# Fourier mixing and SwiGLU in one kernel: the two filter products of batches 2 to 7 summed on GpSimd before the middle inverse, and their mixing spread over 125 slots

## The chip, the cores and the metric

The kernel runs on one core of one Trainium2 chip. The metric is the time of one execution on the device, in microseconds (us). Before the change it took 990.07 us (median of three runs, 989.37 to 992.18).

The engines are named as in the profile. PE is the matmul engine, and PEld its weight loads. DVE is VectorE, ACT is ScalarE, POOL is GpSimd, and SP is SyncE. SP only issues DMA transfers here. The program gives each engine its instructions in an order, and in the traces here an instruction that has to wait, or a long one, holds up what stands behind it: in the changed kernel a copy on DVE starts at 596.56 us, when the 0.69 us operation placed ahead of it has ended.

## The reference, cut to what matters

```python
def _attn_ref(x, filt_r, filt_i):            # x: 8 x 3008 x 256
    X = np.fft.rfft(x, axis=1)
    F = (filt_r + 1j * filt_i)[None, :, :]
    return np.fft.irfft(X * F, n=x.shape[1], axis=1).astype(np.float32)

def _moe_ref(x, w_gate, w_val, w_out, rms_g): # x: 24064 x 256, d_ff 1536
    rms = np.sqrt(np.mean(x * x, axis=-1, keepdims=True) + 1e-06)
    xn = x / rms * rms_g
    g = xn @ w_gate
    silu = g * (1.0 / (1.0 + np.exp(-g)))
    return (silu * (xn @ w_val) @ w_out).astype(np.float32)
```

The first function mixes the 3008 tokens of each batch with a filter in the frequency domain. The second is an RMS norm and a gated feed-forward network on every token.

## The kernel before

The transform of length 3008 = 47 x 64 is done as small matmuls in fp16. One batch passes through these stages, named by the PSUM tile that PE writes:

- `psa`: first forward stage. ACT copies it out, and it is stored to a scratch tensor `z_tmp` in HBM.
- `psb`: second forward stage, from `t2`, which is loaded from `z_tmp`. It has 16 units of two columns of the filter.
- Filter: DVE makes two products of `psb`, `s1` with the real part of the filter and `s2` with the imaginary part.
- `psi`: middle inverse, four matmuls a unit. ACT copies it out, and it is stored to `g_tmp`.
- `psn`: last inverse, from `t4`, which is loaded from `g_tmp`. ACT makes `y` and the square `sq` of it.
- `psq`: row sums of the squares. DVE and POOL turn them into the factor of the norm, and POOL makes `xn`.

```python
def b_unit(b, i):
    ps = bank(0 if b else i % 2, "psb").rearrange("p (a d) -> p a d", a=2)   # bank 0: psM, "mx"
    for u in range(2):
        k = 2 * i + u
        nc.tensor.matmul(ps[:, u, :], wb[:, k, :], st[b]["t2"][k // KC][:, k % KC, :], ...)
    ...
    eng.tensor_tensor(out=s1, in0=ps, in1=f1, op=ALU.mult)     # DVE for b > 0
    eng.tensor_tensor(out=s2, in0=ps, in1=f2, op=ALU.mult)

def bi_unit(b, i):
    ...
    for u in range(2):
        for q in range(2):
            nc.tensor.matmul(ps[:, u, :], wi[:, 2 * i + u, q, :], s12[q][:, u, :],
                             start=(q == 0), stop=(q == 1))
```

The feed-forward part is a stream of 576 slots: 8 batches x 6 blocks of 512 tokens (the last of a batch has 448) x 12 slices of the hidden width. In a slot `gv` makes `pg` and `pv` (four 512-column matmuls), ACT makes `sg = silu(pg)` and DVE makes `hh = pv * sg`. Two slots later `down` multiplies `hh` into `po`. After the twelfth slice ACT copies one half of `po` out and DVE the other. There is only one pair of `po` buffers.

```python
psG = ...tile_pool(name="psG", bufs=2, ...)    # pg
psV = ...tile_pool(name="psV", bufs=2, ...)    # pv
psO = ...tile_pool(name="psO", bufs=1, ...)    # po0, po1
psM = ...tile_pool(name="psM", bufs=2, ...)    # "mx": psa, psb, psi, psn, psq

def down(b, m, jt):
    ...
    if jt == JT - 1:
        nc.scalar.activation(out=o3[:, 0:2, :], in_=po[0], func=AXT.Copy)
        nc.vector.tensor_copy(out=o3[:, 2:4, :], in_=po[1])          # m < 5
```

The mixing of batch b is laid between the slots of batch b-1 by a plan that says which unit goes into which slot. Inside a slot the order is `gv`, then the planned units, then `down`:

```python
for b in range(1, B):
    t = (b - 1) * 72                                   # first slot of batch b - 1
    a0, b0, bs = (8, 24, 6) if b == 1 else (0, 16, 8)
    ...                                                # a_unit, z_store, t2_load
    for i in range(16):
        s0 = t + b0 + bs * i // 4                      # one psb unit every second slot
        at(s0, b_unit, b, i)
        at(s0 + 3, bi_unit, b, i)
        if i % 2 == 1:
            at(s0 + 4, g_store, b, i // 2)
    for c in range(4):
        at(t + 54, t4_load, b, c)
    for m in range(6):
        norm_plan(b, m, t + 57 + 8 * m)
for i in range(len(items) + 4):
    gv(*items[i])
    for fn, a in plan.get(i, ()):
        fn(*a)
    down(*items[i - 2])                                # guards and o_store cut
```

## Time and profile before

| view | number |
|---|---|
| busy PE, DVE, ACT, POOL (page) | 92%, 60%, 61%, 26% of 988.5 us |
| PE in the stretch 549 to 662 us, one batch | busy 110.8 of 112.8 us, clock 1.00 |
| time from one batch's last output copy to the next's, batches 1 to 6 | 112.6 to 113.8 us |
| one group of four 256-column or two 512-column matmuls (timeline) | 0.434 us to the next |

The page gives the busy time, share of the span and number of instructions of each engine. Its row PEclk cuts the span into 40 slices and gives the granted clock of PE in tenths.

```profile
PE 910.5 (92%) x6287; PEld 576.3 (58%) x6287; DVE 594.6 (60%) x961; ACT 606.1 (61%) x1061; POOL 256.1 (26%) x219
PEclk8557989999999999999999999999999999999999
```

The windows view cuts the span where one batch's last output copy ends and the next one's. Its columns are the window, its length, the busy time of PE, PEld, DVE, ACT and POOL (with instructions), the granted clock, the DMA share and GB/s. Here is one batch of the kernel before:

```profile
549.37:662.18 112.81, 110.84 (x782) 70.87 (x781) 70.97 (x118) 73.25 (x132) 27.74 (x22) 1.00 0.48 112
```

PE is busy for 98% of it, and no other engine for as much as two thirds. The kernel is bound by PE: what PE does not have to do is time gained, and any hole on PE is time lost.

The timeline of PE in the kernel before has the start, the duration, the operation and the count of a group. In square brackets stand the idle time before the group and what ended it. This is a whole slot with a `psi` unit in it:

```profile
500.07 0.60 PE L239 MATMUL psi<-s,wi 128*128 128x256 f16 x4
500.50 0.60 PE L376 MATMUL po<-wo,hh 128*128 128x256 f16 x4
500.94 0.59 PE L360 MATMUL pg<-xn,wg 128*128 128x512 f16 x2
501.37 0.59 PE L360 MATMUL pv<-xn,wv 128*128 128x512 f16 x2
```

The durations overlap; it is the starts that count. The groups start 0.43 us apart, so 0.109 us goes to one 256-column matmul, and a slot takes 1.30 us without mixing work.

The waits of PE in the kernel before have the waiting tile, what it waited for, the total, the number of times and the longest:

```profile
PE psb L213 <- DMA t<-z_tmp: 17.6, 8, 4.8
PE psi L239 <- DVE s L231: 2.6, 6, 0.4
PE po L376 <- DVE o L382: 0.6, 1, 0.6
```

The first `psb` of each batch waits for its load from `z_tmp`; for batches 2 to 7 together that is 9.1 of the 17.6 us.

One hole in batch 1's mixing shows what a long wait costs beyond itself:

```profile
128.16 0.61 PE L213 MATMUL psb<-t,wb 96*128 96x256 f16 x2 [3.67 <-DMA t<-z_tmp]
128.57 1.06 PE L376 MATMUL po<-wo,hh 128*128 128x256 f16 x4
129.42 1.06 PE L360 MATMUL pg<-xn,wg 128*128 128x512 f16 x2
```

After 3.67 us without work the groups start 0.85 us apart instead of 0.43, until 134 us.

Last, the queue of SP in the kernel before:

```profile
519.73 8.42 SPq L256 DMA_DIRECT2D t<-g_tmp  x16
```

Issuing the 16 transfers of a batch's `t4` load keeps SP busy for 8.42 us, and whatever is queued behind them is issued that much later.

### The profile page before, as it was taken

What the parts mean: (1) busy time and instruction counts of PE and PEld (TensorE: products, weight loads), DVE (VectorE), ACT (ScalarE), POOL (GpSimd) and SP (SyncE); (2) the same over time, 40 slices, a digit from 0 to 9 for tenths busy, and PEclk for the clock granted to TensorE, in tenths of its full rate; (3) what the DMA queues carried; (4) which work ended last, traced back from release to release, by engine and by line L of the source; (5) the groups of instructions that cost most, each with busy time, mean ns of one, the idle gap of its engine ahead of it and who ended that gap; (6) DMA issues with size and microseconds to landing.
All of it is one profiled execution on the core that took longest, in us unless ns stands there. A gap on an engine that the chain in (4) does not pass through costs nothing.

```text
span 988.5 us, 17348 instructions
## 1 busy us (share of the span) xinstructions
PE 910.5 (92%) x6287; PEld 576.3 (58%) x6287; DVE 594.6 (60%) x961; ACT 606.1 (61%) x1061; POOL 256.1 (26%) x219
## 2 busy tenths in 40 slices
PE   3447989999999999999999999999999999999997
PEld 1224646665666566665666566665666556666654
DVE  6623468546775477645775467655775467655554
ACT  7334845576656865676656765577656756566543
POOL 3564231033301342032401233031411312023300
PEclk8557989999999999999999999999999999999999
DMA  8869573335632474325723375425724343322211
GB/s 195 145 136 165 123 144 80 110 97 113 152 94 79 113 167 96 102 78 140 154 52 120 94 160 115 109 67 112 163 76 125 88 118 89 99 67 62 44 43 40
DMA packets 94837, 106.98 MB, mean 108 GB/s; under 512 B 17112, under 2 KB 69464, under 8 KB 94560
## 3 DMA queue, kind: packets, MB, share of 16 engines
q1 hardware_dynamic: 85104, 87.92, 34.1%
q0 software_dynamic: 9552, 17.77, 12.1%
q8 instruction: 49, 0.80, 0.3%
q14 instruction: 36, 0.29, 0.1%
q10 hardware_dynamic: 96, 0.20, 0.1%
HBM read 70.62 MB, written 49.90 MB: 122 GB/s over the span
## 4 chain that ended last, share of the span: by engine, by line
PE 75%; DMA 9%; ACT 5%; issue 4%; DVE 2%; POOL 2%; SPq 1%; ACTq 0%; DVEq 0%; POOLq 0%
PE po L376 22%; PE pg L360 21%; PE pv L360 21%; PE psi L239 5%; DMA t<-z_tmp 3%; PE psb L213 3%; DMA fi<-in_filt_i_dram 2%; DMA z_tmp<-t 2%; PE psn L270 2%; ACT sq L277 1%; ACT t L194 1%; PE psa L192 1%; SPq L202 1%; DMA xc<-in_x_dram 1%; ACT y L275 1%
## 5 line engine op out<-in xcount | busy, mean ns | idle before, releaser
L365 DVE TENSOR_TENSOR hh<-pv,sg 128x512 f16<-128x512 f32 (+1 forms) x576 | 390.7, 678 | 330.3 <-ACT sg L364 212.8
L364 ACT ACTIVATE sg<-pg 128x512 f16<-128x512 f32 (+1 forms) x576 | 341.1, 592 | 294.9 <-PE pg L360 274.9
L376 PE MATMUL po<-wo,hh 128*128 128x256 f16 x2304 | 349.8, 273 | 3.2 <-DVE o L382 0.6
L360 PE MATMUL pg<-xn,wg 128*128 128x512 f16 (+1 forms) x1152 | 339.9, 377 | 0.0
L360 PE MATMUL pv<-xn,wv 128*128 128x512 f16 (+1 forms) x1152 | 339.1, 376 | 0.0
L376 PEld LDWEIGHTS <-hh 128*128 128x128 f16 x2304 | 221.0, 98 | 93.2 <-issue 14.9
L345 POOL TENSOR_TENSOR xn<-y,rb 128x1024 f16<-128x1024 f32 x46 | 132.2, 2875 | 313.3 <-DMA rb<-r_tmp 220.8
L360 PEld LDWEIGHTS <-wv 128*128 128x128 f16 x1152 | 113.1, 98 | 132.6 <-issue 3.0
L290 POOL TENSOR_TENSOR rho<-u,mhalf 128x4 f32<-128x4 f32 x48 | 48.8, 1017 | 327.8 <-DVE u L288 327.8
L360 PEld LDWEIGHTS <-wg 128*128 128x128 f16 x1152 | 112.9, 98 | 14.1 <-issue 0.6
L244 ACT ACTIVATE t<-psi 96x512 f16<-96x512 f32 x128 | 75.7, 593 | 32.1 <-PE psi L239 30.5
L239 PEld LDWEIGHTS <-wi 128*128 128x128 f16 x512 | 51.5, 102 | 55.9 <-issue 13.1
L230 DVE TENSOR_TENSOR s<-psb,fr 128x512 f16<-128x512 f32 x112 | 76.3, 681 | 10.3 <-PE psb L213 10.3
L231 DVE TENSOR_TENSOR s<-psb,fi 128x512 f16<-128x512 f32 x112 | 76.2, 680 | 0.0
L275 ACT ACTIVATE y<-psn,gsb 128x512 f32<-128x512 f32 x94 | 65.4, 696 | 9.5 <-PE psn L270 4.1
L213 PE MATMUL psb<-t,wb 96*128 96x256 f16 x256 | 52.6, 292 | 18.6 <-DMA t<-z_tmp 17.6
L239 PE MATMUL psi<-s,wi 128*128 128x256 f16 x448 | 67.3, 273 | 2.6 <-DVE s L231 2.6
L194 ACT ACTIVATE t<-psa 128x512 f16<-128x512 f32 x96 | 58.0, 615 | 5.1 <-PE psa L192 2.7
L277 ACT ACTIVATE sq<-psn 128x512 f16<-128x512 f32 x94 | 56.7, 603 | 0.0
L213 PEld LDWEIGHTS <-wb 96*128 96x128 f16 x256 | 25.2, 105 | 40.3 <-issue 17.5
L192 PE MATMUL psa<-xc,wa 128*128 128x512 f16 x96 | 37.3, 405 | 10.6 <-DMA xc<-in_x_dram 8.9
L270 PEld LDWEIGHTS <-t 128*128 128x128 f16 x376 | 29.2, 99 | 21.0
(55 smaller groups left out, 331.6 us busy)
## 6 DMA issues: line engine op xcount, KB each, us to landing
out_dram<-o SPq DMA_DIRECT2D x88, 256.0 KB, 3.6
z_tmp<-t SPq DMA_DIRECT2D x128, 96.0 KB, 2.2
t<-z_tmp SPq DMA_DIRECT2D x32, 384.0 KB, 5.9
g_tmp<-t SPq DMA_DIRECT2D x64, 192.0 KB, 2.4
t<-g_tmp SPq DMA_DIRECT2D x126, 96.0 KB, 2.5
rb<-r_tmp SPq DMA_DIRECT2D x46, 256.0 KB, 4.0
xc<-in_x_dram POOLq DMA_DIRECT2D x56, 192.0 KB, 6.1
out_dram<-o SPq DMA_DIRECT2D x8, 192.0 KB, 3.0
```

Source lines behind the costliest of these rows:

```text
L194: nc.scalar.activation(out=dst, in_=src, func=AXT.Copy)
L213: nc.tensor.matmul(ps[:, u, :], wb[:, k, :], st[b]["t2"][k // KC][:, k % KC, :], start=True, stop=True)
L230: eng.tensor_tensor(out=s1, in0=ps, in1=f1, op=ALU.mult)
L231: eng.tensor_tensor(out=s2, in0=ps, in1=f2, op=ALU.mult)
L239: nc.tensor.matmul(ps[:, u, :], wi[:, 2 * i + u, q, :], s12[q][:, u, :], start=(q == 0), stop=(q == 1))
L244: nc.scalar.activation(out=st[b]["t3"][c][:, 2 * r:2 * r + 2, :], in_=ps[0:KR], func=AXT.Copy)
L275: nc.scalar.activation(out=y[:, dh, :], in_=ps, func=AXT.Identity, scale=gsb[:, dh:dh + 1])
L345: nc.gpsimd.tensor_tensor(out=xv, in0=yv, in1=rv.unsqueeze(1).to_broadcast([P, 2, 4, P]), op=ALU.mult)
L360: nc.tensor.matmul(ps[:, 0:w], wt[:, dt_, ts(jt, P)], xn[:, dt_, 0:w], start=(dt_ == 0), stop=(dt_ == 1))
L364: nc.scalar.activation(out=sg[:, 0:w], in_=pg[:, 0:w], func=AXT.Silu)
L365: nc.vector.tensor_tensor(out=hh[:, 0:w], in0=pv[:, 0:w], in1=sg[:, 0:w], op=ALU.mult)
L376: nc.tensor.matmul(po[s4 // 2][:, s4 % 2, :], hh[:, ts(s4, P)], wo[:, jt, :], start=(jt == 0 and s4 % 2 == 0), stop=(jt == JT - 1 and s4 % ...
```

## The change

The middle inverse multiplies `s1` by one matrix and `s2` by a second one, which is the first with its two halves of 64 rows exchanged and one sign turned. If the halves of `s2` are exchanged when it is made, and the sign is put into the filter, one matrix serves both, and `s1 + s2` can be formed before the matmul. That takes `psi` from four matmuls a unit to two. DVE has to make `s2` in two crosswise halves of 64 partitions, and POOL does the sum. To give the longer chain room, the mixing of batches 2 to 7 is spread: `psb` comes every fourth slot instead of every second, `psi` six slots after its `psb` instead of three, and from the first `psa` to the last store to `g_tmp` one batch now takes 125 slots. PSUM is divided anew: one "mx" buffer for `psa`, `psi` and `psn`, and one "mb" buffer for `psb` and `psq`, where two "mx" buffers served all five.

The core of the diff (small helpers, batch 0's and the x loads' placing cut):

```diff
-                    wi[HALF + q, 0, 1, qq] = -(gr, gi)[cols][0]
+                    wi[HALF + q, 0, 1, qq] = (gr, gi)[cols][0]
...
-    psM = ctx.enter_context(tc.tile_pool(name="psM", bufs=2, space=bass.MemoryType.PSUM))
+    psM = ctx.enter_context(tc.tile_pool(name="psM", bufs=1, space=bass.MemoryType.PSUM))
+    psB = ctx.enter_context(tc.tile_pool(name="psB", bufs=1, space=bass.MemoryType.PSUM))
...
+            if b > 1:
+                nc.vector.tensor_tensor(out=s1, in0=ps, in1=f1, op=ALU.mult)
+                st[b]["s"][i] = (s1, s2, ps, f2)
+                return
...
+    def swap_unit(b, i, h):
+        s1, s2, ps, f2 = st[b]["s"][i]
+        a, e = slice(HALF * h, HALF * h + HALF), slice(HALF - HALF * h, P - HALF * h)
+        nc.vector.tensor_tensor(out=s2[a], in0=ps[e], in1=f2[e], op=ALU.mult)
+        if h:
+            s = ssp.tile([P, 2, D], FP16, tag="s", name="s")
+            nc.gpsimd.tensor_tensor(out=s, in0=s1, in1=s2, op=ALU.add)
+            st[b]["s"][i] = (s,)
...
-            for q in range(2):
-                nc.tensor.matmul(ps[:, u, :], wi[:, 2 * i + u, q, :], s12[q][:, u, :],
-                                 start=(q == 0), stop=(q == 1))
+            for q in range(n):
+                nc.tensor.matmul(ps[:, u, :], wi[:, 2 * i + u, q, :], ss[q][:, u, :],
+                                 start=(q == 0), stop=(q == n - 1))
...
-            a0, b0, bs = (8, 24, 6) if b == 1 else (0, 16, 8)
+            a_at = ([8 + i for i in range(12)] if b == 1 else
+                    [24 + 2 * i for i in range(12)] if b == 2 else [t - 77 + 4 * i for i in range(12)])
+            b_at = [24 + 3 * i // 2 if b == 1 else t - 20 + 4 * i for i in range(16)]
...
-                at(t + b0 - 3 + c if c < 3 else t + b0 + 8, t2_load, b, c)
+                at(b_at[0] - 3 + c if c < 3 else b_at[4] + 1, t2_load, b, c)
...
+                if b > 1:
+                    at(s0 + 1, swap_unit, b, i, 0)
+                    at(s0 + 2, swap_unit, b, i, 1)
+                lag = 6 if b > 1 else 3
+                at(s0 + lag, bi_unit, b, i)
...
-                at(t + 54, t4_load, b, c)
+                at(b_at[15] + (9 if b > 1 else 8), t4_load, b, c)
-                norm_plan(b, m, t + 57 + 8 * m)
+                norm_plan(b, m, t + 52 + 8 * m if b > 1 else t + 57 + 8 * m, 4, 3)
```

In `bi_unit`, `n` is 1 for batches 2 to 7 and 2 for the first two, which keep the old product. A planned `swap_unit` or `sq_unit` goes to the front of its slot, ahead of the other planned units. Where the text says "swaps" below, it means the two `swap_unit` operations. `norm_plan` now takes the gap between the two halves of `psn` and the lag from the second to `psq`, and `sq` is made one slot after its `psn`.

More of the change, by code (lines that the diff above doesn't have):

```diff
@@ L133 @@
     sp = ctx.enter_context(tc.tile_pool(name="sp", bufs=3))
+    ssp = ctx.enter_context(tc.tile_pool(name="ssp", bufs=2))
     t3p = ctx.enter_context(tc.tile_pool(name="t3p", bufs=3))
@@ L179, in bank @@
     def bank(i, name):
-        pool, tag = ((psM, "mx"), (psG, "pg"), (psV, "pv"))[i]
+        pool, tag = ((psM, "mx"), (psG, "pg"), (psV, "pv"), (psB, "mb"))[i]
         return pool.tile([P, 512], FP32, tag=tag, name=name)
@@ L209, in b_unit @@
     def b_unit(b, i):
-        ps = bank(0 if b else i % 2, "psb").rearrange("p (a d) -> p a d", a=2)
+        ps = bank(3 if b else (0, 1, 3)[i % 3], "psb").rearrange("p (a d) -> p a d", a=2)
         for u in range(2):
@@ L232, in b_unit @@
         st[b]["s"][i] = (s1, s2)
+    def swap_unit(b, i, h):
[6 more added lines that the diff above has]
+            st[b]["s"][i] = (s,)
     def bi_unit(b, i):
-        s12 = st[b]["s"].pop(i)
+        ss = st[b]["s"].pop(i)
         ps = bank(0 if b else 2, "psi").rearrange("p (a d) -> p a d", a=2)
+        n = len(ss)
         for u in range(2):
-            for q in range(2):
-                nc.tensor.matmul(ps[:, u, :], wi[:, 2 * i + u, q, :], s12[q][:, u, :],
-                                 start=(q == 0), stop=(q == 1))
+            for q in range(n):
+                nc.tensor.matmul(ps[:, u, :], wi[:, 2 * i + u, q, :], ss[q][:, u, :],
+                                 start=(q == 0), stop=(q == n - 1))
         c, r = divmod(i, 2)
@@ L266, in n_unit @@
         y = st[b]["y"][m]
-        ps = psM.tile([P, 512], FP32, tag="mx", name="psn")
+        ps = bank(0, "psn")
         for q in range(4):
@@ L276, in n_unit, with sq_unit @@
                              scale=gsb[:, dh:dh + 1])
-        nc.scalar.activation(out=st[b]["sq"][m][:, dh, :], in_=ps, func=AXT.Square)
+        st[b]["sq"][m, dh] = ps
+    def sq_unit(b, m, dh):
+        nc.scalar.activation(out=st[b]["sq"][m][:, dh, :], in_=st[b]["sq"].pop((m, dh)),
+                             func=AXT.Square)
     def q_unit(b, m):
         sq = st[b]["sq"].pop(m)
-        ps = psM.tile([P, 4], FP32, tag="mx", name="psq")
+        ps = psB.tile([P, 4], FP32, tag="mb", name="psq")
         for q in range(4):
@@ L416, in f_dup @@
         nc.vector.tensor_copy(out=fr[c][HALF:P], in_=fr[c][0:HALF])
-        nc.scalar.activation(out=fi[c][HALF:P], in_=fi[c][0:HALF], func=AXT.Copy)
+        nc.scalar.activation(out=fi[c][HALF:P], in_=fi[c][0:HALF], func=AXT.Copy, scale=-1.0)
     def wi_group(g):
@@ L426, in wi_group @@
         nc.scalar.activation(out=wi[:, k, 0, :], in_=ps[:, lo:4, :], func=AXT.Copy, scale=S_INV_B)
-        for p0, sign in ((0, 1.0), (HALF, -1.0)):
+        for p0 in (0, HALF):
             nc.vector.tensor_scalar(out=wi[p0:p0 + HALF, k, 1, :],
-                                    in0=ps[HALF - p0:P - p0, lo:4, :], scalar1=sign * S_INV_B,
+                                    in0=ps[HALF - p0:P - p0, lo:4, :], scalar1=S_INV_B,
                                     scalar2=None, op0=ALU.mult)
@@ L508 @@
         w_load(2)
-        n_unit(0, 1, 0)
-        n_unit(0, 1, 1)
+        for dh in range(2):
+            n_unit(0, 1, dh)
+            sq_unit(0, 1, dh)
         for c in range(NXC):
@@ L517, in at, with norm_plan @@
         def at(slot, fn, *a):
-            plan.setdefault(slot, []).append((fn, a))
-        def norm_plan(b, m, s0):
-            at(s0, n_unit, b, m, 0)
-            at(s0 + 1, n_unit, b, m, 1)
-            at(s0 + 3, q_unit, b, m)
-            at(s0 + 5, rho_move, b, m)
-            at(s0 + 10, xn_unit, b, m)
+            todo = plan.setdefault(slot, [])
+            if fn in (sq_unit, swap_unit) and a[0]:
+                todo.insert(0, (fn, a))
+            else:
+                todo.append((fn, a))
+        def norm_plan(b, m, s0, gap, lag):
+            for dh in range(2):
+                at(s0 + gap * dh, n_unit, b, m, dh)
+                at(s0 + gap * dh + (b > 0), sq_unit, b, m, dh)
+            q0 = s0 + gap + lag
+            at(q0, q_unit, b, m)
+            at(q0 + 2, rho_move, b, m)
+            at(q0 + 6, xn_unit, b, m)
         at(1, q_unit, 0, 1)
@@ L530 @@
         for m in range(2, 6):
-            norm_plan(0, m, 2 + (m - 2) * 9)
+            norm_plan(0, m, 2 + (m - 2) * 9, 2, 2)
         for b in range(1, B):
             t = (b - 1) * 72
-            a0, b0, bs = (8, 24, 6) if b == 1 else (0, 16, 8)
+            a_at = ([8 + i for i in range(12)] if b == 1 else
+                    [24 + 2 * i for i in range(12)] if b == 2 else [t - 77 + 4 * i for i in range(12)])
+            b_at = [24 + 3 * i // 2 if b == 1 else t - 20 + 4 * i for i in range(16)]
             for i in range(12):
-                at(t + a0 + i, a_unit, b, i)
+                at(a_at[i], a_unit, b, i)
                 if i % 3 == 2:
-                    at(t + a0 + i + 1, z_store, b, i // 3)
+                    at(a_at[i] + 1, z_store, b, i // 3)
             for c in range(4):
-                at(t + b0 - 3 + c if c < 3 else t + b0 + 8, t2_load, b, c)
+                at(b_at[0] - 3 + c if c < 3 else b_at[4] + 1, t2_load, b, c)
             for i in range(16):
-                s0 = t + b0 + bs * i // 4
+                s0 = b_at[i]
                 at(s0, b_unit, b, i)
-                at(s0 + 3, bi_unit, b, i)
+                if b > 1:
[3 more added lines that the diff above has]
+                at(s0 + lag, bi_unit, b, i)
                 if i % 2 == 1:
-                    at(s0 + 4, g_store, b, i // 2)
+                    at(s0 + lag + 1, g_store, b, i // 2)
             if b + 1 < B:
                 for c in range(NXC):
-                    at(t + 20 + 4 * c, x_load, b + 1, c)
+                    at(a_at[3 * c + 2] + 1, x_load, b + 1, c)
             for c in range(4):
-                at(t + 54, t4_load, b, c)
+                at(b_at[15] + (9 if b > 1 else 8), t4_load, b, c)
             for m in range(6):
-                norm_plan(b, m, t + 57 + 8 * m)
+                norm_plan(b, m, t + 52 + 8 * m if b > 1 else t + 57 + 8 * m, 4, 3)
         stores = {}
```

## The prediction

> **What bounds the kernel now.** The tensor engine. In the table of equal stretches PE is busy 97 to 99% of every 100 us from 200 to 900 us at granted clock 1.00; DVE 60 to 65%, ACT 61 to 66%, POOL 20 to 28%. In the timeline a slot (one gate/up/down step) takes 1.30 us, with a middle-inverse unit of four matmuls 1.74: PE streams. The repeated hole (waits of PE) is the first psb of each batch waiting for its z_tmp load: 1.8, 1.2, 1.9, 1.0, 1.1, 2.1 us for batches 2 to 7.
>
> **Gains, all on the critical path.** 96 units lose two of four 256-column matmuls: 0.44 us becomes 0.22, in all 192 x 0.109 = 20.9 us. The z stores now run far ahead of the loads: the 9.1 us of psb waits lose their old cause. Sum -30 us.
>
> **Work moved, hidden.** 96 more DVE operations of 0.68 us (+65 us) and 96 POOL adds (estimated 1.25 us, as batch 0's POOL products; +120 us) have room: the add has four slots before its matmul.
>
> **Costs**, paid whole, as PE works in order.
> 1. *t2 behind t4 on the SP queue, batches 3 to 7.* In the instruction order the first t2 load of batch b+1 is issued after the 16 t4 loads of batch b, three slots before psb needs it. Chain from the slot of the last psi: copy out 2.0, g store 2.4, 16 issues 7.4 to 8.4, t2 load 3.4 to 4.4 us: about 16.5 us. The psb is wanted after six slots, 9.1 us. Stall 7.5 us, five times. The Trainium skill, "TensorE: Matmul & The Clock Gate", section "Part 1: The HAM clock gate", says that an idle window of some 3.4 us halves the PE clock; this trace agrees: after a 3.7 us hole at 124 us, matmul groups take 0.85 instead of 0.43 us until 134. Estimated at 2.3 us each. +49 us.
> 2. *One buffer instead of two for "mx", batch 1's norm against batch 2's mixing (slots 57 to 102).* Each of 12 psi units awaits the square of the psn before it, on ACT after silu: about 1.0 us each, +12 us. Six psb follow psq on "mb" and await u on DVE: +6 us. Batch 1's first xn is late on POOL, behind an add: +3 us.
> 3. *Slots 11 to 46:* psa behind psi or psn on "mx": 7 x 0.7 + 3 x 1.5 us and one psb: about +9 us.
> 4. *Later batches:* psq awaits the second swap product, about 0.3 us, 30 times: +8 us.
>
> Sum +87 - 30: about 1047 us; I shade it to 1043.
>
> **What would show each step.** psi matmuls fall from 448 to 256 on s tiles. PE waits: psb on the t2 load, five times 6 to 9 us, each followed by a lower PEclk; psi on ACT sq 12 times about 1 us between 170 and 260 us; psq on DVE. The time between two batches, 112.8 us now, grows to about 119.
>
> **What would make it wrong.** If issuing the t4 loads is faster than in the trace, or the t2 load lands sooner, cost 1 shrinks and the result nears 1000 us. Without cost 1 the others roughly cancel the gain. The half-clock stretches may differ. Slower POOL adds would make psi wait on POOL too.
>
> Predicted 1043 us (1010 to 1065); faster by over 2%: 0.06, within 2%: 0.13, slower: 0.81.

## The result, and the profile after

The changed kernel is correct and takes 1064.65 us (median of four runs, 1063.94 to 1068.52). The kernel before took 989.72 us in the same rounds (four runs, 988.75 to 992.18). The ratio is 1.0761, with a 95% interval of 1.0729 to 1.0794: slower. A ratio is always the mean time of one kernel's fast runs over that of the other's of the same rounds, so it is not quite the ratio of the medians quoted. The profiled execution of the changed kernel is its slowest run, 1068.5 us, with a span of 1066.3 us; its first slot starts at 83.8 us, 3.7 us later than in the profiled run of before, which is not counted as an effect and was not followed up.

The page of the kernel after, with the group of the new operation on POOL (its columns: busy us and mean ns of one, then the idle time before):

```profile
PE 910.7 (85%) x6095; PEld 558.3 (52%) x6095; DVE 679.7 (64%) x1057; ACT 622.0 (58%) x1061; POOL 364.8 (34%) x315
PEclk8567989989998999989998999989999999999999
L246 POOL TENSOR_TENSOR s<-s,s 128x512 f16<-128x512 f16 x96 | 110.5, 1151 | 440.4 <-DVE s L243 399.0
```

PE did 192 matmuls less, as intended, yet its share fell from 92 to 85% of a longer span. DVE grew to 64% and POOL to 34%, so no engine is full. Dips stand in the row of the clock, one in nearly every batch. The sum on POOL takes 1.15 us, a little under the 1.25 that was estimated; the Trainium skill, "GPSIMD Engine Reference", section 3.1, gives about 2.6 cycles an element at 1.2 GHz for such an operation, from which 512 elements would be estimated at 1.11 us, so the trace agrees. No `psi` waits for the sum anywhere in the waits of PE. Nor did POOL's new work slow DVE: one `hh` took 678 ns on average before and 681 after (both pages).

Two windows of the kernel after, one batch and the stretch behind one of the dips:

```profile
615.24:738.69 123.45, 110.16 (x749) 67.83 (x748) 85.21 (x134) 75.35 (x132) 46.08 (x38) 0.96 0.45 102
579.00:584.10 5.10, 5.10 (x19) 2.37 (x17) 2.08 (x3) 1.63 (x3) 0.00 (x0) 0.51 0.62 178
```

A batch takes 123.5 instead of 112.8 us. PE is idle for 13 us of it, against 2. For 5.1 us it has work all the time and gets half its clock.

The waits of PE in the kernel after name the holes:

```profile
PE psb L215 <- DMA t<-z_tmp: 46.6, 8, 7.9
PE po L396 <- DVE o L402: 15.4, 23, 0.7
...
PE psi L255 <- ACT sq L296: 11.0, 13, 1.3
PE psq L304 <- DVE s L243: 9.0, 30, 0.6
PE psb L215 <- DVE u L308: 5.4, 7, 0.9
PE po L396 <- DVE o L405: 3.7, 5, 0.7
PE psa L194 <- ACT t L260: 3.2, 7, 0.5
PE pg L380 <- POOL xn L365: 2.8, 1, 2.8
PE psa L194 <- ACT sq L296: 2.5, 2, 1.3
```

(The line left out is batch 0's, before the stream starts.) Five of the eight waits for `z_tmp` belong to batches 3 to 7: 5.93, 6.97, 6.41, 7.95 and 7.25 us. The queue of SP shows where that of batch 5 comes from:

```profile
564.67 0.32 SPq L263 DMA_DIRECT2D g_tmp<-t  x1
567.08 7.26 SPq L272 DMA_DIRECT2D t<-g_tmp  x16
574.39 1.00 SPq L208 DMA_DIRECT2D t<-z_tmp  x2
```

The 16 loads of batch 4's `t4` need its last `g_tmp` store, and can only begin at 567.08. The load that batch 5's first `psb` needs stands behind them in the same queue and is issued at 574.39. PE meanwhile (timeline of the kernel after):

```profile
571.87 0.39 PE L286 MATMUL psn<-wai,t 128*128 128x128 f16 x4
578.67 0.58 PE L215 MATMUL psb<-t,wb 96*128 96x256 f16 x2 [6.41 <-DMA t<-z_tmp]
579.05 1.06 PE L396 MATMUL po<-wo,hh 128*128 128x256 f16 x4
579.90 1.06 PE L380 MATMUL pg<-xn,wg 128*128 128x512 f16 x2
...
584.52 0.60 PE L380 MATMUL pg<-xn,wg 128*128 128x512 f16 x2
```

From 579.05 to 584.52 it does seven groups. At 0.434 us each they would take 3.04 us, so the slow stretch costs another 2.43 us, and 0.16 more for the `psb` before it. Counted in the same way, the stretches behind the five holes cost 2.0, 2.3, 2.6, 2.0 and 2.2 us. A shorter hole, the one behind batch 1's first `xn`, did it too (same view):

```profile
232.74 1.01 PE L380 MATMUL pg<-xn,wg 128*128 128x512 f16 x2 [2.77 <-POOL xn L365]
233.55 1.06 PE L380 MATMUL pv<-xn,wv 128*128 128x512 f16 x2
```

The second largest line of the waits, `po` on the output copy, is a wait that the kernel before had once. It now comes 28 times (23 for the full blocks, 5 for the last, shorter block of a batch). DVE and PE around the end of a block, in the kernel after:

```profile
595.18 0.62 DVE L385 TENSOR_TENSOR hh<-pv,sg 128x448 f16<-128x448 f32 x1 [0.42 <-PE po L396]
595.84 0.69 DVE L243 TENSOR_TENSOR s<-psb,fi 64x512 f16<-64x512 f32 x1
596.56 0.69 DVE L402 COPY o<-po 128x512 f32<-128x512 f32 x1
597.30 0.38 PE L396 MATMUL po<-wo,hh 128*128 128x256 f16 x2 [0.73 <-DVE o L402]
```

DVE does the product `hh`, then a swap, and only then the copy that frees the one `po` buffer, for which the next block's first `down` waits. A block ends every 12 slots and a swap comes every fourth slot in the same place, so once they meet they always meet: the slot number is 1 modulo 4 for both. The pair of `po` matmuls was due at 596.42 (0.22 us after the pair before it, which started at 596.20), and came at 597.30, 0.88 us late. The wait listed is 0.73. The modelled end of the last matmul before a hole covers its first 0.15 us or so (a 256-column matmul is drawn 0.273 us long, but in the stream the next one starts 0.109 us after it). So about 0.16 us, called the tail below, is added to each PE wait where waits are turned into time.

### Where the time went

The time per batch can be added up in the middle of the run. A later experiment (e7) ran the spread schedule with the old product and with nearly no hole, at 109.6 us a batch. 16 units of two 256-column matmuls less are 3.5 us, which leaves 106.1 us of pure stream.

| part of one batch, batches 2 to 5 | us |
|---|---|
| stream | 106.1 |
| `psb` behind the `t4` loads, 7.1 + 0.16 | 7.3 |
| half clock after it | 2.3 |
| `po` on the output copy, 5 x 0.86 | 4.3 |
| `psq` on the swap, 1.9 + 6 x 0.16 | 2.9 |
| sum | 122.9 |
| measured | 122.3 to 123.5 |

The kernel before takes 113.1 us a batch on average (batches 1 to 6): 109.6, plus 1.7 us for its `z_tmp` hole, 0.6 for one `psi` that waits for its product, and some 1.5 us in short holes that the list of waits leaves out. Three times a batch a `psa` and the `po` behind it each start about 0.25 us late: in its timeline at 550.49 and 550.98 us, where the groups ahead of them give 550.25 and 550.71. The trace of the changed kernel has no such holes in batches 2 to 5. Batch 0's and 1's slots, where batch 1's norm meets batch 2's mixing, lose further: the first batch's end moves from 209.3 to 240.2 us, partly because more of batch 2's work lies in front of it, and batch 1's period is 129.8 us.

### The profile page after: what moved, and what is told of

It is laid out like the page before. It is cut to its first block, busy times and chain, and to the rows that moved or that the text cites. A ratio compares the mean times of both kernels' runs of the same rounds, so it can differ in the third digit from the quotient of the medians.

```text
span 1066.3 us, 17416 instructions
## 1 busy us (share of the span) xinstructions
PE 910.7 (85%) x6095; PEld 558.3 (52%) x6095; DVE 679.7 (64%) x1057; ACT 622.0 (58%) x1061; POOL 364.8 (34%) x315
## 4 chain that ended last, share of the span: by engine, by line
PE 62%; DMA 11%; DVE 11%; issue 8%; ACT 4%; POOL 3%; SPq 2%; DVEq 0%; POOLq 0%; ACTq 0%
PE po L396 19%; PE pg L380 18%; PE pv L380 16%; DVE hh L385 4%; DVE s L243 4%; DMA t<-z_tmp 3%; PE psb L215 2%; DMA fi<-in_filt_i_dram 2%; DVE o L402 2%; ACT sg L384 2%; PE psn L286 2%; PE psi L255 2%; SPq L272 2%; PE psa L194 2%; DMA t<-g_tmp 1%
## 5 line engine op out<-in xcount | busy, mean ns | idle before, releaser
L396 PE MATMUL po<-wo,hh 128*128 128x256 f16 x2304 | 358.3, 276 | 19.8 <-DVE o L402 15.4
L380 PE MATMUL pg<-xn,wg 128*128 128x512 f16 (+1 forms) x1152 | 344.8, 382 | 2.8 <-POOL xn L365 2.8
L380 PE MATMUL pv<-xn,wv 128*128 128x512 f16 (+1 forms) x1152 | 343.5, 380 | 0.0
L396 PEld LDWEIGHTS <-hh 128*128 128x128 f16 x2304 | 224.2, 99 | 128.8 <-issue 33.7
L246 POOL TENSOR_TENSOR s<-s,s 128x512 f16<-128x512 f16 x96 | 110.5, 1151 | 440.4 <-DVE s L243 399.0
L243 DVE TENSOR_TENSOR s<-psb,fi 64x512 f16<-64x512 f32 x192 | 132.2, 688 | 5.9
L215 PE MATMUL psb<-t,wb 96*128 96x256 f16 x256 | 53.6, 295 | 52.6 <-DMA t<-z_tmp 46.6
L223 DVE TENSOR_TENSOR s<-psb,fr 128x512 f16<-128x512 f32 x96 | 65.5, 682 | 38.5 <-PE psb L215 38.5
L260 ACT ACTIVATE t<-psi 96x512 f16<-96x512 f32 x128 | 75.6, 593 | 17.5 <-PE psi L255 13.5
L255 PEld LDWEIGHTS <-wi 128*128 128x128 f16 x320 | 31.6, 103 | 65.9 <-issue 16.9
L255 PE MATMUL psi<-s,wi 128*128 128x256 f16 x256 | 46.4, 273 | 11.0 <-ACT sq L296 11.0
L194 PE MATMUL psa<-xc,wa 128*128 128x512 f16 x96 | 37.5, 405 | 15.3 <-DMA xc<-in_x_dram 8.6
```

The source lines that it names most:

```text
L223: nc.vector.tensor_tensor(out=s1, in0=ps, in1=f1, op=ALU.mult)
L243: nc.vector.tensor_tensor(out=s2[a], in0=ps[e], in1=f2[e], op=ALU.mult)
L246: nc.gpsimd.tensor_tensor(out=s, in0=s1, in1=s2, op=ALU.add)
L255: nc.tensor.matmul(ps[:, u, :], wi[:, 2 * i + u, q, :], ss[q][:, u, :], start=(q == 0), stop=(q == n - 1))
L260: nc.scalar.activation(out=st[b]["t3"][c][:, 2 * r:2 * r + 2, :], in_=ps[0:KR], func=AXT.Copy)
L380: nc.tensor.matmul(ps[:, 0:w], wt[:, dt_, ts(jt, P)], xn[:, dt_, 0:w], start=(dt_ == 0), stop=(dt_ == 1))
```

## The experiments

Two theories stood after the result. Theory A: the loss is in the placing, a handful of orders in queues and slots, and each can be undone alone. Rival B: the loss is in the new work itself, DVE and POOL having too little room, or in the halved number of "mx" buffers, so that moving orders about only moves the holes. All ten kernels gave correct results. They ran on three chips, each beside the kernel before on the same chip, where that took 992.1 us (e1 to e4), 993.3 (e5 to e8) and 992.6 (e9 and e10), against 989.7 beside the changed kernel, whose chip is not on record. A comparison with the changed kernel may therefore go across chips: it is given from the medians, and where it matters from the ratios too, which make it 2 to 4 us larger.

### e1_t2_early: the `t2` loads five slots earlier

```diff
-                at(b_at[0] - 3 + c if c < 3 else b_at[4] + 1, t2_load, b, c)
+                at(b_at[0] - (3 if b < 3 else 8) + c if c < 3 else b_at[4] + 1, t2_load, b, c)
```

> The changed kernel with one edit: for batches 3 to 7 the first three t2 loads are issued five slots earlier, ahead of the 16 t4 loads in the SP queue. Queue-order theory: the five psb waits on the t2 load (5.9, 7.0, 6.4, 8.0, 7.3 us in the changed kernel) and the half-clock stretch after each (about 2.4 us) go: about 45 us less, near 1020 us; granted clock up. Rival (DVE and POOL are simply too full, the t2 wait is only where the backlog shows): the time moves to other waits, result above 1050 us.

Measured: 1035.15 us, ratio 1.0446 (1.0413 to 1.0479), against 992.14 of before. The queue order is confirmed: waits of `psb` for `z_tmp` fell from 46.6 us in 8 to 8.7 in 3, at the first `psb` of batches 0, 1 and 2. It fell 15 us short of what was expected, and the waits of PE in this run say why: `psn` now waits for `t4`, a wait that had been hidden behind the one removed.

```profile
PE psn L286 <- DMA t<-g_tmp: 13.5, 5, 4.2
```

Two of these holes in the timeline of this run, each with a group that follows it:

```profile
441.11 0.38 PE L286 MATMUL psn<-wai,t 128*128 128x128 f16 x4 [3.38 <-DMA t<-g_tmp]
441.99 0.59 PE L380 MATMUL pg<-xn,wg 128*128 128x512 f16 x2
...
558.83 0.39 PE L286 MATMUL psn<-wai,t 128*128 128x128 f16 x4 [4.17 <-DMA t<-g_tmp]
560.30 1.06 PE L380 MATMUL pg<-xn,wg 128*128 128x512 f16 x2
```

A hole of 3.38 us left the clock alone, and one of 4.17 us was followed by groups at half speed. The Trainium skill, "TensorE: Matmul & The Clock Gate", section "Part 1: The HAM clock gate", puts the idle window that throttles the clock at about 3.4 us, and calls this window free-running. The two holes here agree with it. The hole of 2.77 us in the changed kernel does not: it was shorter than 3.38 us and lowered the clock. Nor do holes in later runs: those of 1.92 us (e5), 2.58 (e6), 2.18 (e7) and 1.96 (e8) were each followed by some 3.4 us at a clock of 0.50, and those of 2.12 (e5) and 2.61 (e8) were not. So length alone does not decide in this range.

### e2_copy_first: the swap after the output copy

Only in the slots where a block ends, the swap is emitted behind `down`.

```diff
+            late = [] if i % JT != 1 else [u for u in plan.get(i, ()) if u[0] is swap_unit]
             for fn, a in plan.get(i, ()):
-                fn(*a)
+                if (fn, a) not in late:
+                    fn(*a)
             ... down(*items[i - 2])
+            for fn, a in late:
+                fn(*a)
```

> The changed kernel with one edit: in the slots in which a block's down projection ends (every twelfth), the swap product is issued on DVE after the copy of po, not before it. Theory (the swap ahead of the copy holds the only po buffer): the 28 waits of po on the DVE copy, 19.1 us in all, fall to a few us; some psq waits on the swap grow by 0.3 us; 12 to 17 us less, near 1050 us. Rival (DVE as a whole is too busy, order is indifferent): the waits move to psq or pv, result within 5 us of the changed kernel.

Measured: 1049.41 us, ratio 1.0567 (1.0538 to 1.0597), 15 us below the changed kernel by the medians and 19 by the ratios. Of the 28 waits of `po` on the output copy one is left in the waits of PE, as short as the one of the kernel before:

```profile
PE po L396 <- DVE o L402: 0.4, 1, 0.4
```

Nothing but the order of two DVE operations in one slot was changed, so that order caused the other 27. Not all of the some 24 us came back, because `psq` now waits for the swap, which ends later: 16.2 us in 30 instead of 9.0.

### e3_norm1_phase: batch 1's norm one slot earlier

```diff
-                norm_plan(b, m, t + 52 + 8 * m if b > 1 else t + 57 + 8 * m, 4, 3)
+                norm_plan(b, m, t + (52 if b > 1 else 56) + 8 * m, 4, 3)
```

> The changed kernel with one edit: the norm of batch 1 starts at slot 56 in place of 57, so that it falls in the same phase of four slots as the later batches have. Theory (one mx buffer, wrong phase): the 12 psi waits on ACT sq (about 11 us), 6 psb waits on u (5 us) and the late first xn (2.8 us) go; about 1 to 2 us come back as a wait for t4 and 2 us as psq waits: 15 to 19 us less, near 1048 us. Rival (one mx buffer is too few whatever the phase): under 5 us less.

Measured: 1049.54 us, ratio 1.0575 (1.0554 to 1.0597), 15 us less by the medians and 18 by the ratios. In the waits of PE, `pg` on `xn` is gone, `psb` on `u` fell from 5.4 us in 7 to 0.4 in 1, and `psi` on `sq` is one wait where there were 13:

```profile
PE psi L255 <- ACT sq L296: 1.3, 1, 1.3
```

The number of buffers is the same in both kernels. With one "mx" buffer, a `psi` unit that comes directly behind a `psn` waits for the square to be made; one slot earlier, the square is done in time. So it was the phase, and the buffer count alone was not the cause. Other waits grew: `po` on the copy from 19.1 us in 28 to 21.9 in 32, and `psq` on the swap from 9.0 in 30 to 10.9 in 36. This is where rival B first fails.

### e4_old_product: the schedule of the change with the product of before

The signs are put back, `s1` and `s2` are made back to back on DVE, `psi` takes four matmuls, and there are no swaps and no sums. Slots and buffers stay those of the change.

```diff
-            if b > 1:
-                nc.vector.tensor_tensor(out=s1, in0=ps, in1=f1, op=ALU.mult)
-                st[b]["s"][i] = (s1, s2, ps, f2)
-                return
...
-                    at(s0 + 1, swap_unit, b, i, 0)
-                    at(s0 + 2, swap_unit, b, i, 1)
```

> The changed kernel's schedule and buffers with the old product: s1 and s2 computed back to back on DVE, no swap, no POOL add, two matmuls a column in the middle inverse. If the sum itself is worth its 20.9 us and only the schedule loses: 20 us more, near 1085 us. If the swap products give the saving back through DVE waits (psq on swap 9 us, po on the copy 19 us), these waits go and the result is within 10 us of the changed kernel, possibly below it: 1055 to 1068 us.

Measured: 1044.14 us, ratio 1.0518 (1.0496 to 1.054). It is 20 us *faster* than the changed kernel (24 by the ratios), though PE has 20.9 us more to do, and lower than either expectation. `psq` on a swap does not occur, and `po` on DVE's copy once (0.4 us). The waits of PE that remain are those of the schedule:

```profile
PE psb L215 <- DMA t<-z_tmp: 45.2, 8, 7.3
```

So the loss has two parts of about the same size. The schedule with its new buffers, without the sum, loses about 52 us (1044.1 against 992.1). The swaps and the sum, placed as they are, cost 41 to 45 us to save 20.9, which is the 20 to 24 us above and the 20.9 together.

### e5_three: e1, e2 and e3 together

> The edits of the first three experiments together: t2 loads ahead of the t4 loads, the po copy ahead of the swap, batch 1's norm in the common phase. If the three causes are separate, their gains add: 1065 minus 30, 15 and 15, so about 1005 us, still slower than before, with waits of psn on t4 (about 13 us and half-clock) and of psq on the swap (about 16 us) left. If they overlap (one cause behind all three), the result stays above 1020 us.

Measured: 994.21 us against 993.31 of before, ratio 1.0012 (0.9978 to 1.0045): the same. The three gains add up and a little more: 30 + 15 + 15 = 60 us one by one and 70 together by the medians, 31 + 19 + 18 = 68 and 74 by the ratios. The `t4` waits of e1 fit part of the extra: they fall from 13.5 to 9.2 us in 5, none over 2.1, and where two of them were followed by half clock in e1, one is here, behind a hole of 1.92 us:

```profile
421.20:424.50 3.30, 3.30 (x13) 1.58 (x11) 1.61 (x3) 1.54 (x3) 0.00 (x0) 0.50 0.72 210
```

This stretch cost 1.7 us. `psq` on the swap has grown to 19.7 us in 36.

### e6_all: the norm of all batches in that phase, and `psq` after `down` as well

The diff is against e5.

```diff
-            late = [] if i % JT != 1 else [u for u in plan.get(i, ()) if u[0] is swap_unit]
+            late = [u for u in plan.get(i, ())
+                    if (u[0] is swap_unit and i % JT == 1) or (u[0] is q_unit and u[1][0])]
...
-                norm_plan(b, m, t + (52 if b > 1 else 56) + 8 * m, 4, 3)
+                norm_plan(b, m, t + 56 + 8 * m, 4, 3)
```

> The three edits together and two more: the norm of all batches starts four slots later (so that psn finds t4 landed), and psq is issued after the down projection of its slot (so that the swap product ahead of it has time to end). Theory: the psn waits on t4 fall from about 13 to under 2 us, the psq waits from about 16 to under 6 us; result near 980 us, faster than before by about 1%. If the sum can't pay even without these waits, it stays above 995 us.

Measured: 969.26 us, ratio 0.9765 (0.9731 to 0.9798): faster than the kernel before, and 11 us less than was expected. `psq` waits only 5.0 us in 12, and `t4` once, 2.6 us. The two new edits were not run apart. One batch in the windows of this run, and below it one of the next run, e7:

```profile
553.37:660.66 107.29, 106.44 (x750) 67.45 (x748) 84.65 (x134) 75.41 (x131) 46.24 (x37) 1.00 0.51 118
```

DVE does 84.7 us of work a batch, as in the changed kernel (85.2), and PE is now busy for 99% at clock 1.00. DVE and POOL had room for the new work. Rival B falls with this run.

### e7_old_fixed: the same orders with the old product

This is e4 with the `t2` loads of e1 and the norm of all batches at t + 56.

> The changed kernel's spread schedule with the old product (as in the run that put it back), with the t2 loads ahead of t4 and the norm of all batches at slot 56 of its period. No swap, no add. Theory (the schedule's loss of 54 us is the queue order and the phase, nothing else): the t2 waits, half-clock stretches and psi waits on sq go, result 978 to 990 us. The difference to the run with all repairs and the sum is what the sum is worth once nothing waits: 21 us at most, less where DVE still delays PE.

Measured: 981.58 us, ratio 0.9886 (0.9854 to 0.9918).

```profile
558.83:668.42 109.59, 109.53 (x781) 70.68 (x780) 70.66 (x118) 75.86 (x131) 28.20 (x21) 1.00 0.50 115
```

PE has no hole left in this batch. A well ordered spread schedule is worth about 1% by itself; its interval lies below 1. The sum is worth 981.6 - 969.3 = 12 us on top of it, less than the 20.9 us that PE saves. The `psq` waits that e6 still has account for about 7 of the 9 us that are missing (5.0 us, and 12 x 0.16); the rest was not resolved.

### e8_sum_only: only the sum, in the schedule of before

`s1` and both swaps follow each other on DVE, POOL adds, `psi` takes two matmuls a unit, four slots behind `psb` instead of three. A first build with four buffers for the sum did not fit into SBUF; this one has two.

```diff
+            if b > 1:
+                nc.vector.tensor_tensor(out=s1, in0=ps, in1=f1, op=ALU.mult)
+                for h in range(2):
+                    a, e = slice(HALF * h, HALF * h + HALF), slice(HALF - HALF * h, P - HALF * h)
+                    nc.vector.tensor_tensor(out=s2[a], in0=ps[e], in1=f2[e], op=ALU.mult)
+                s = ssp.tile([P, 2, D], FP16, tag="s", name="s")
+                nc.gpsimd.tensor_tensor(out=s, in0=s1, in1=s2, op=ALU.add)
...
-                at(s0 + 3, bi_unit, b, i)
+                lag = 4 if b > 1 else 3
+                at(s0 + lag, bi_unit, b, i)
```

> The kernel before, its schedule of one unit in two slots and two mx buffers, with only the product changed: s1 and two swap products back to back on DVE, the sum on POOL, one matmul a column, psi one slot later. Estimate from the traces: two slots then need 5 DVE operations of about 0.65 us, 3.25 us, against 3.04 us of PE (3.26 us with the old product): DVE sets the pace and the sum wins nearly nothing. Expected 985 to 1000 us. If DVE doesn't bind, the full 21 us show: near 970 us.

Measured: 1008.26 us, ratio 1.0163 (1.0122 to 1.0204), slower than was expected; by the 2% rule the verdict is unclear, though the whole interval lies above 1. The timeline of DVE in this run:

```profile
379.51 1.29 DVE L375 TENSOR_TENSOR hh<-pv,sg 128x512 f16<-128x512 f32 x2
380.72 0.68 DVE L222 TENSOR_TENSOR s<-psb,fr 128x512 f16<-128x512 f32 x1
381.42 1.39 DVE L225 TENSOR_TENSOR s<-psb,fi 64x512 f16<-64x512 f32 x2
382.84 1.29 DVE L375 TENSOR_TENSOR hh<-pv,sg 128x512 f16<-128x512 f32 x2
```

Two slots hold two `hh`, one `s1` and two swaps, and repeat after 3.33 us (379.51 to 382.84) without a gap on DVE. PE needs 3.04 us for them: two slots of 1.30, `psb` 0.22 and `psi` 0.22. Where `psb` comes every second slot, DVE sets the pace. The waits of PE also name `psb` behind ACT's square (9.6 us in 7) and behind ACT's copy (8.2 in 12), so the pace need not be the whole loss. The sum did not pay in the old schedule, and the spreading was not a mistake as such; whether every third slot would do was not tested.

### e9_early and e10_all_again: the early slots, with e6 repeated beside it

e9 is e6 with batch 1's `psa` units a little earlier and spaced, and batch 2's `psa` units after `down`. With other slots a `t2` load would have read `z_tmp` before the store. e10 is e6 again.

```diff
-            a_at = ([8 + i for i in range(12)] if b == 1 else
+            a_at = ([6, 7, 8, 9, 10, 12] + [14 + i for i in range(6)] if b == 1 else
...
+                    or (u[0] is a_unit and u[1][0] == 2)]
```

> The repaired kernel with two more edits for the slots 6 to 46, where the change's single mx buffer makes psa wait: psa of batch 1 keeps out of the two slots that hold a psn, and psa of batch 2 is issued after the down projection of its slot. Theory (term 3 of the prediction, about 9 us in all): psa waits on ACT sq 2.5 us go, those on ACT t 3.2 us fall below 1 us, and about 0.16 us more each for the tail of a matmul that a hole uncovers: 4 to 6 us less than the repaired kernel on the same chip. If these holes were hidden behind the wait of the first psb for its load, nothing changes.

> The repaired kernel (all five edits, as run before) once more, on the same chip as the run with the early slots mended, to compare the two: 966 to 973 us, about 2.3% below before.

Measured in five rounds on one chip, against 992.58 us of before: e9 964.88 us, ratio 0.9728 (0.9696 to 0.9759); e10 971.43 us, ratio 0.9783 (0.9753 to 0.9814). The two lines of `psa` on `sq` and on `t` that e10 still has (2.5 us in 2 and 3.2 us in 7) are absent from e9's waits, and e9 is 6.5 us shorter. Its first batch ends at 222.7 us where e10's ends at 230.5; later periods are the same within 0.3 us. So e9 is the best version found: 2.7% below the kernel before. Its interval lies beyond 2%, and e10's reaches to 0.9814 (its verdict is unclear by the 2% rule, while that of e6, the same kernel, is faster).

## Why the prediction was right or wrong

The direction and the main mechanism were right. The size was 21.7 us short (1043 against 1064.65), and the result lies at the very end of the range of 1010 to 1065. The sum of costs was short by one whole term, the waits of `po` on the output copy (23.6 us), and by several small tails. The table takes the terms as the prediction put them, against the trace of the changed kernel; waits carry the 0.16 us of covered time where that is said.

| term | predicted, us | measured, us |
|---|---|---|
| two `psi` matmuls less a unit | -20.9 | holds: 192 matmuls less |
| old `psb` waits lose their cause | -9.1 | gone but for 1.0 at batch 2; for batches 3 to 7 another wait took their place |
| 1. `t2` behind `t4`, five waits | 37.5 | 34.5 listed, 35.3 with tails |
| 1. half clock after each | 11.5 | 11.1 (2.2 each) |
| 2. `psi` on the square, 12 times | 12 | 9.7 listed, 11.6 with tails |
| 2. `psb` on `u` | 6 | 5.0 listed, 6 with tails |
| 2. batch 1's first `xn` | 3 | 2.8, and 2.6 of half clock after it |
| 3. slots 11 to 46 | 9 | about 8 listed, 10 with tails |
| 4. `psq` on the swap, 30 times | 8 | 9.0 listed, 13.8 with tails |
| `po` on the output copy | not in the sum | 19.1 listed, 23.6 with tails |
| batch 1's first `psb` on its `t2` | not in the sum | +1.8 |

- *What bounds the kernel.* Right. PE is busy for 98% of a batch before, and removing its holes later made the kernel faster each time.
- *"Work moved, hidden."* This is the step that failed. The sum on POOL is hidden: no `psi` waits for it. The added DVE operations were judged by DVE's share of busy time, and that held for DVE as a whole (64% busy in the end). It did not hold for their place in DVE's order. The prediction listed `psq` as a victim of the swap and overlooked the output copy, a rare operation (once in 12 slots) that holds the only `po` buffer. It is the missing term: 23.6 us, and e2 makes 27 of those 28 waits vanish by changing only the order. For the swaps and the sum together the prediction booked 8 us (its cost 4); e4 puts them at 41 to 45, of which these waits and those of `psq` are 37.
- *Cost 1, `t2` behind `t4`.* Right in place, number, length (predicted 7.5 us each, measured 5.9 to 8.0) and in the half clock (predicted 2.3 us each, measured 2.0 to 2.6). e1 confirms the cause.
- *Costs 2 and 3.* Right in place and nearly in size. It was put down to "one buffer instead of two"; e3 keeps the one buffer, moves the norm by one slot and loses the waits. The buffer made the wait possible, and the phase made it happen.
- *Cost 4.* The 30 waits are right. The size is short because 30 holes lose 0.16 us each beyond what is listed. The prediction took listed waits as whole; over the some 60 waits of its terms that is another 10 us.
- *"The sum is 87, less 30."* The half-clock stretch after the late `xn` (2.6 us) was also missed: the prediction gave this hole of 2.8 us none.
- *"Shade it to 1043."* The own sum said 1047. No number stood behind the shading, and it went the wrong way.
- *"Without cost 1 the others roughly cancel the gain."* Wrong. By the prediction's own terms that would have been 8 us above the kernel before; e1 is 43 us above it. Behind the removed wait stood the `t4` wait, 13.5 us with two half-clock stretches, and the output copies stood beside it.
- *"The time between two batches grows to about 119."* It grew to 122.3 to 123.5 us. The 4.3 us of output copies are more than the whole difference at the lower end.

The terms of the table, measured, sum to more than the 75 us that were lost: about 119 us of costs with tails, less 30 for the gains, is 89. The rest is a gain that nobody predicted: the late `psi`, `psa` and `po` of the kernel before, 13 us over batches 1 to 6 in its trace, do not occur in batches 2 to 5 of the changed kernel. It hid part of the shortfall, so that the 18 us between the prediction's own sum of 1047 and the result are less than the costs it missed; that is luck. No run isolates this gain.

## What to carry to other kernels

When an engine that is not full gets new work, do not stop at its share: list every operation in its order that somebody waits for, the rare ones too, and look at which of them the new work stands in front of, above all where a single buffer is handed back. Periodic work on fixed slots meets in the same phase each time, so one slot of shift or one exchange in order can remove a dozen holes at once; here four such moves turned a loss of 7.6% into a gain of 2.3%, with the same arithmetic. Expect a second wait behind each one that is removed, and count a hole of PE of some 2 us or more as possibly 1.7 to 2.6 us longer than it is, for the half clock that followed many of them here.

## What the Trainium skill lacked or had wrong

- "DMA: Bandwidth & Descriptors", section "Issuing engines are not separate DMA queues", calls the time to initiate a DMA "usually small relative to the DMA itself". One by one the trace agrees (0.45 to 0.53 us to issue, 2.3 us from issue to landing for the `t4` loads). But in the changed kernel 16 issues in a row took 7.3 to 8.4 us on one queue, and a load queued behind them made PE wait 5.9 to 8.0 us in each of five batches. The page does not say that a later, urgent load pays for the issues before it.
- "TensorE: Matmul & The Clock Gate", section "Part 1: The HAM clock gate", gives about 3.4 us of idle time as the threshold. Holes from 3.38 us up fit (3.38 us did not lower the clock; 3.67, 3.70 and all longer ones in the stream did), but shorter ones of 1.92 (e5), 1.96 (e8), 2.18 (e7), 2.58 (e6) and 2.77 us (the changed kernel) lowered it too, which a whole idle window of 3.4 us cannot explain, while others of 2.12 (e5) and 2.61 us (e8) did not. What decides between them was not isolated.
- "Perfetto Trace Analysis", section "Identifying Performance Opportunities", under "Optimization Strategy", says that consistent bubbles can mean too little SBUF or PSUM. Here a repeated bubble (12 of `psi` on the square, 11.0 us listed with one more) went with the same number of buffers when the work moved by one slot (e3). The section could add phase as a cause.
- The same page, section "Tensor Engine Instruction (MATMUL, LD_WEIGHTS)", says that the end of a matmul is estimated. Here a 256-column matmul is drawn with 273 ns and issues every 109 ns, so each listed idle time of PE is about 0.16 us shorter than the time lost. The page gives no number for this.
- "VectorE: DVE Perf Modes", section "Two Vector instructions with no wait between them", tells when an operation is held until the ones before have finished, but gives no price. Here products that exchange the partition halves start 0.70 to 0.71 us apart (e8), and those that keep them 0.60 us apart in the kernel before; no run isolates it.
